# One loop over all eight head groups on TensorE, VectorE and ScalarE of a cached-attention decode kernel

## The chip, the cores and the metric

One core of a Trainium2 chip runs the kernel. The metric is the device time of one execution in microseconds, as the median of several runs. The engines are named TensorE (PE in the profile; PEld is its weight load), VectorE (DVE), ScalarE (ACT), GpSimd (POOL) and SyncE (SP, which here issues nearly all DMAs). A profile also has the granted TensorE clock.

## What is computed

One decode step of a transformer block for four batch rows with one token each: adaptive layer norm from a condition `c`, attention over a cache of 4096 keys and values for 32 heads, and a gated MLP. The bytes are in the two caches (134 MB each, bf16).

```python
mod = (_silu(c) @ w_mod).reshape(c.shape[0], 6, 1, -1)      # sa, ca, ga, sb, cb, gb
h = _layernorm(x) * (1 + ca) + sa
# _A_ref: B, Sq, D = 4, 1, 512; H, Sk, Dh = 32, 4096, 128
q = (h @ wq).reshape(B, Sq, H, Dh).transpose(0, 2, 1, 3)
scores = einsum('bhqd,bhkd->bhqk', q, k_cache) * Dh ** (-0.5)
o = einsum('bhqk,bhkd->bhqd', softmax(scores), v_cache)
x = x + ga * (o.transpose(0, 2, 1, 3).reshape(B, Sq, H * Dh) @ wo)
h = _layernorm(x) * (1 + cb) + sb
# _B_ref: z = gelu(h @ w_in); z1, z2 = halves, z2 layer-normed
# (z1 * (w_sp * z2 + b_sp)) @ w_out
x = x + gb * _B_ref(h, ...)
```

## The kernel before

The 32 heads are eight groups `g` of four heads. A *quad* `i = 4 g + b` is one group of one batch row: its keys fill one SBUF tile `kt[i % 2]` of 128 partitions by 16,384 bf16 (4 MiB: 32 partitions for each head, 128 keys on each), its values one tile `vt[i % 2]`. There are 32 quads, and two buffers for K and two for V.

The prologue loads `w_mod` and `wq` into the two V buffers, computes the modulation, the first layer norm, and `qbc`, the queries of all heads repeated over the partitions: eight products into PSUM, each cast by ScalarE. Then come the quads. In the step of quad `i`:

- SP issues the load of K of quad `i+1` and of V of quad `i`, and in the third quad of a group (`b == 2`) the group's slice of `wo` into `wo_g`.
- `diagonal(i-2)`: four small fp32 products pick each head's own block out of `osb`, the P.V result of quad `i-2`.
- `scores(i, half)`, twice: VectorE multiplies half of the K tile in place with the query (8192 elements a partition, 4.4 us), and TensorE adds the products up in groups with 16 products by the identity into a PSUM bank `s_ps[half]`.
- `project(i-2)`, between the halves: VectorE divides by the sum of exponentials `z`, into `oT`.
- `fold(i, half)`: VectorE's last reduction of the score sums into `S`.
- `softmax(i)`: maximum over each head (with two 32x32 transposes), Exp on ScalarE, and `P4`, the exponentials masked by head.
- `values(i-1)`: `z` by one fp32 product, then 32 products of P by V into `po_ps`; ScalarE copies that to `osb`.
- `apply(i-2)`, for the last quad of a group only: the product of the group's four `oT` with `wo_g`, added up in one PSUM bank `attn_ps`.

After the last quad `values_last` multiplies P and V in 128 small products, quad by quad of keys as the parts of the last V tile land, and goes to `attn_ps` with `wo_l`; then come the second layer norm, the MLP (weights `win`, `wout`) and the output.

Nothing is scheduled by a compiler. `Program` records each operation with the regions that it reads and writes, derives the waits (`depend`, `order`), and writes each engine's stream in recorded order (`run`). Each operation may raise one semaphore. Only TensorE has a loop: a pass is four quads, `passno = (i - 2) // B`, seven passes over quads 2 to 29; quads 0, 1, 30 and 31 are written out. TensorE inside its loop may wait only on semaphores whose names begin with `pe_`, since those counts repeat in every pass: at the end of a pass TensorE lowers each by what the pass added (five of them: `pe_act`, `pe_dve`, `pe_v0`, `pe_v1`, `pe_wo`). An operation whose exact predecessor raises no semaphore that it may read waits for a later one on the same engine that does (line 115). VectorE, ScalarE and SP are written out for all 32 quads.

The end has its own arrangements. For quad 31 the K tile is loaded in two halves with semaphores of their own (`load_k`, lines 400 to 405), so that the first half can be multiplied before the second lands; the V tile comes in five parts (`load_v`). `keep_busy(4)` puts four idle products ahead of the last scores (lines 645 to 646). `softmax(30)` is recorded after the products of quad 31 instead of in its own quad (lines 651 to 656). The six loads of late weights (`wo_l`, `win`, `wout`) are issued behind the V parts; `load_sp` lets loads whose names begin with `wo` or `wi` wait for the load eight places earlier in SP's stream.

Of the kernel before, what the change touches and what calls it, by code (L numbers as in the profile page):

```python
# [30 lines left out]
class Op:  # L31
    def __init__(self, eng, emit, reads, writes, sem, passno, done):
        self.eng, self.emit, self.reads, self.writes = eng, emit, reads, writes
        self.sem, self.passno, self.done = sem, passno, done
        self.pos = self.count = None
        self.clock, self.waits, self.dma = {}, [], False


class Program:
# [3 lines left out]
    def __init__(self, nc):  # L43
        self.nc = nc
        self.ops, self.by_eng = [], {}
        self.passno = None
        self.last_write, self.readers = {}, {}

    def add(self, eng, emit, reads, writes, sem=None, done=True, dma=False, after=()):
        reads, writes = list(reads), list(writes)  # L50
        for r in reads[:]:
            if r.space == bass.MemoryType.PSUM:
                reads.remove(r)
                writes.append(r)
        op = Op(eng, emit, [region(r) for r in reads], [region(w) for w in writes],
                sem or eng, self.passno, done)
# [9 lines left out]
    def depend(self, op):  # L66
# [7 lines left out]
        for r in op.reads:  # L74
            for w, reg in self.last_write.get(r[0], ()):
                if hit(r, reg):
                    deps.add((w, "raw"))
# [7 lines left out]
        for r in op.reads:  # L85
            self.readers.setdefault(r[0], []).append((op, r))
# [13 lines left out]
    def order(self):  # L100

        known = {}
        for op in self.ops:
# [6 lines left out]
            for key, d in sorted(need.items(), key=lambda kd: -kd[1].idx):  # L110
                if clock.get(key, -1) >= d.pos:
                    continue
                if not d.dma:
                    lst = self.by_eng[d.eng]
                    d = next(o for o in lst[d.pos:] if o.done and self.tells(o.sem, op))
                op.waits.append(d)
                for k, v in d.clock.items():
                    clock[k] = max(clock.get(k, -1), v)
            op.clock = dict(clock)
            op.clock[("dma", id(op)) if op.dma else op.eng] = op.pos  # L120
            if not op.dma:
                clock[(op.eng, "issued")] = op.pos

    def tells(self, sem, op):

        own = sem.startswith("pe_")
        return op.eng == "PE" and (own or op.passno is None) or op.eng != "PE" and not own

    def call(self, eng, name, *args, sem=None, done=True, after=(), **kw):
        outs = [kw[k] for k in OUTS if k in kw]  # L130
        ins = [v for k, v in kw.items() if k not in OUTS and isinstance(v, bass.AP)]
        if not outs:
            outs, args_in = [args[0]], args[1:]
            ins += [a for a in args_in if isinstance(a, bass.AP)]
        return self.add(
            eng, lambda e: getattr(e, name)(*args, **kw), ins, outs, sem=sem, done=done, after=after,  # L136
        )

    def load(self, eng, sem, out, in_, after=()):
        return self.add(  # L140
            eng, lambda e: e.dma_start(out=out, in_=in_), [], [out], sem=sem, dma=True, after=after,  # L141
        )

    def run(self, alloc, passes, engines):


        self.order()
        sems, total, count = {}, {}, {}
        for op in self.ops:
            if op.done:  # L150
                step = 16 if op.dma else 1
                total[op.sem] = total.get(op.sem, 0) + step
                op.count = total[op.sem]
                sems.setdefault(op.sem, None)
        for name in sems:
            sems[name] = alloc(name)
        loops = [[o for o in self.by_eng["PE"] if o.passno == p] for p in range(passes)]
        own = {s for s in sems if s.startswith("pe_")}
        step, wait = {}, []
        for pos in range(len(loops[0])):  # L160
            vals = [{d.sem: d.count for d in lp[pos].waits} for lp in loops]
            for v in vals:
                assert set(v) <= own, v
            wait.append(vals)
        for s in own:
            rows = [
                (p, pos, wait[pos][p][s]) for pos in range(len(wait)) for p in range(passes)
                if s in wait[pos][p]
            ]
            per = {}  # L170
            for p, pos, v in rows:
                per.setdefault(pos, {})[p] = v
            diffs = {
                (b - a) // 1 for d in per.values() for p in range(passes - 1)
                if p in d and p + 1 in d for a, b in ((d[p], d[p + 1]),)
            }
            assert len(diffs) <= 1, (s, diffs)
            step[s] = diffs.pop() if diffs else 0
        norm = []
        for pos, vals in enumerate(wait):  # L180
            best = {}
            for p, v in enumerate(vals):
                for s, x in v.items():
                    best[s] = max(best.get(s, 0), x - p * step[s])
            norm.append(best)

        def emit(op, eng, waits):
            waits = list(waits)
            for s, v in waits[1:]:
                eng.wait_ge(sems[s], v)  # L190
            inst = op.emit(eng)
# [4 lines left out]

        def plain(op):
            best = {}
            for d in op.waits:
                best[d.sem] = max(best.get(d.sem, 0), d.count)  # L200
            return best.items()

        for name, lst in self.by_eng.items():
            if name != "PE":
                for op in lst:
                    for d in op.waits:
                        assert d.sem not in own, (name, d.sem)
                    emit(op, engines[name], plain(op))
        pe = engines["PE"]
        seen = [o for o in self.by_eng["PE"] if o.passno is None]  # L210
        first = loops[0][0].pos
        for op in seen:
            if op.pos < first:
                emit(op, pe, plain(op))
        with pe.Fori(0, passes):
            for op, w in zip(loops[0], norm):
                emit(op, pe, w.items())
            for s in sorted(own):
                if step[s]:
                    pe.sem_inc(sems[s], -step[s])  # L220
        for op in seen:
            if op.pos > first:
                emit(op, pe, [(s, v - passes * step.get(s, 0)) for s, v in plain(op)])
# [3 lines left out]
def kernel(  # L227
# [111 lines left out]
    prog = Program(nc)  # L339
# [10 lines left out]
    def mm(out, lhsT, rhs, start, stop, done=False, **kw):  # L350
        prog.add(
            "PE", lambda e: e.matmul(out, lhsT=lhsT, rhs=rhs, start=start, stop=stop, **kw),  # L352
            [lhsT, rhs], [out], done=done,
        )

    def mm2(out, lhsT, rhs, start, stop, done=False):

        prog.add("PE", lambda e: e.ldweights(lhsT), [lhsT], [], done=False)  # L358
        moving(out, lhsT, rhs, start, stop, done)

    def moving(out, lhsT, rhs, start, stop, done=False):
        def emit(e):
# [7 lines left out]
        prog.add("PE", emit, [rhs], [out], done=done)  # L370
# [5 lines left out]
    prog.load("ACT", "rows_c", rows[0:B], c)  # L376
    prog.load("ACT", "rows_x", rows[B:2 * B], A_x.rearrange("b s d -> (b s) d"))
    prog.load("ACT", "wb_w", wb_t[:, 0:1], B_w_sp[0:1, 0:1])
    prog.load("ACT", "wb_b", wb_t[:, 1:2], B_b_sp.rearrange("(a b) -> a b", b=1))
    tables = "natural_log_exp_and_others"  # L380
    prog.add("ACT", lambda e: e.preload_act_table_set(tables), [], [], done=False)
# [3 lines left out]
    prog.load("SP", "wm", wm, w_mod.rearrange("(p j) n -> p (j n)", j=J))  # L385
    prog.load("SP", "wq", wq, A_wq.rearrange("(p j) n -> p (j n)", j=J))
# [7 lines left out]
    sp_dma = []  # L394

    def load_sp(sem, out, in_):
        near_end = sem[:2] in ("wo", "wi")
        sp_dma.append(prog.load("SP", sem, out, in_, after=sp_dma[-8:-7] if near_end else ()))

    def load_k(i):  # L400
        a = 0
        for n, part in enumerate((2, 2) if i == NQ - 1 else (1,)):
            b = a + NT * DH // part
            load_sp(f"k{i % 2}" if i < NQ - 1 else f"kl{n}", kt[i % 2][:, a:b], kv_view(A_k_cache, i)[:, a:b])
            a = b

    def load_v(i):
        a = 0
        for n, part in enumerate((2, 4, 8, 16, 16) if i == NQ - 1 else (1,)):
            b = a + NT * DH // part  # L410
            load_sp(
                f"pe_v{i % 2}" if 1 <= i <= 28 else f"v{i}_{n}",
                vt[i % 2][:, a:b], kv_view(A_v_cache, i)[:, a:b],
            )
            a = b

# [5 lines left out]
    for t in (wide, mask4, P4s[0], P4s[1], mxs[0], mxs[1]):  # L422
# [3 lines left out]
    dve("memset", ones_b, 1.0)  # L426
    dve("memset", ones_f, 1.0)
# [4 lines left out]

    def keep_busy(n):
        for _ in range(n):
            mm(big[1], ident, wide, True, True)
# [74 lines left out]
    mm(cut(attn_b, J * B), ident, wide[:, 0:J * B], True, True, skip_group_check=True)  # L510

# [3 lines left out]

    def scores(i, half):
        g, b = divmod(i, B)
        kh = view(kt[i % 2])[:, half * HT:(half + 1) * HT, :]
        dve(
            "tensor_tensor", out=kh, in0=kh,  # L520
            in1=qbc[:, b, g, :][:, None, :].to_broadcast([P, HT, DH]), op=MULT, sem="pe_dve",
        )
        n = DH // DC
        for cc in range(n):
            (mm2 if cc == 0 else moving)(
                s_ps[half], ident, kh[:, :, cc * DC:(cc + 1) * DC], cc == 0, cc == n - 1, cc == n - 1,
            )

    def fold(i, half):
        dve(  # L530
            "tensor_reduce", out=S_t[i % 2][:, half * HT:(half + 1) * HT], in_=s_ps[half],
            axis=AX.X, op=ADD,
        )

    def softmax(i):
# [3 lines left out]
        dve("tensor_reduce", out=mx[:, 0:1], in_=S, axis=AX.X, op=ALU.max)  # L539
# [237 lines left out]
```

## Time and profile before

| | |
|---|---|
| median of 3 runs | 667.03 us (666.99 to 667.08) |
| the profiled execution | 666.79 us, its span 665.0 us |
| busy: TensorE, VectorE, ScalarE | 417.8, 402.7, 41.2 us |
| mean granted TensorE clock | 0.77 |
| HBM read | 282.73 MB |
| K tile, from issue to landing (median) | 25.4 us |
| V tile, from issue to landing (median) | 33.1 us |

The span is what the profile covers; 1.8 us of the execution lie around it. In the timeline each line gives start, duration, engine, line and operation, the tiles written and read, how many, and in brackets the idle time of the engine before it and what ended that. All recorded operations other than matmuls carry the helper's line, so tiles tell them apart.

### The profile page before, as it was taken

What the parts mean: (1) busy time and instruction counts of PE and PEld (TensorE: products, weight loads), DVE (VectorE), ACT (ScalarE), POOL (GpSimd) and SP (SyncE); (2) the same over time, 40 slices, a digit from 0 to 9 for tenths busy, and PEclk for the clock granted to TensorE, in tenths of its full rate; (3) what the DMA queues carried; (4) which work ended last, traced back from release to release, by engine and by line L of the source; (5) the groups of instructions that cost most, each with busy time, mean ns of one, the idle gap of its engine ahead of it and who ended that gap; (6) DMA issues with size and microseconds to landing.
All of it is one profiled execution on the core that took longest, in us unless ns stands there. A gap on an engine that the chain in (4) does not pass through costs nothing.

```text
span 665.0 us, 5909 instructions
## 1 busy us (share of the span) xinstructions
PE 417.8 (63%) x3024; PEld 93.0 (14%) x2065; DVE 402.7 (61%) x475; ACT 41.2 (6%) x115; POOL 3.2 (0%) x17
## 2 busy tenths in 40 slices
PE   2657777565577754576655667656547675567774
PEld 2201111011110101111001111101111110112124
DVE  2166777676556666555766655757655666655662
ACT  1200000000000000000000000000000000000002
POOL 1000000000000000000000000000000000000000
PEclk9977777677887767888766788766778766788895
DMA  9999999999999999999999999999999999999995
GB/s 379 428 424 440 437 422 434 439 434 428 434 436 430 434 434 436 424 436 433 439 428 434 440 426 434 436 434 430 430 440 436 426 434 438 434 430 432 431 416 218
DMA packets 12673, 282.90 MB, mean 425 GB/s; under 512 B 1388, under 2 KB 1908, under 8 KB 3956
## 3 DMA queue, kind: packets, MB, share of 16 engines
q1 hardware_dynamic: 12640, 282.73, 98.8%
q8 instruction: 7, 0.11, 0.1%
q14 instruction: 6, 0.05, 0.0%
q10 hardware_dynamic: 20, 0.01, 0.0%
HBM read 282.73 MB, written 0.00 MB: 425 GB/s over the span
## 4 chain that ended last, share of the span: by engine, by line
DMA 62%; PE 24%; DVE 12%; issue 0%; SPq 0%; ACT 0%; DVEq 0%
DMA kt<-in_A_k_cache_dram 58%; PE bank L363 24%; DVE kt L136 11%; DMA vt<-in_A_v_cache_dram 3%; DMA wout<-in_B_w_out_dram 1%; PE bank L352 0%; SPq L141 0%; DVE S L136 0%; DVE P L136 0%; ACT E L136 0%; DVE mx L136 0%; DVE nm L136 0%; DVE mT L136 0%; DVE hm L136 0%; DVE hb L136 0%
## 5 line engine op out<-in xcount | busy, mean ns | idle before, releaser
L363 PE MATMUL bank<-kt,ident 128*128 128x512 bf16 x1024 | 293.0, 457 | 179.7 <-DVE kt L136 179.7
L136 DVE TENSOR_TENSOR kt<-kt,qbc 128x8192 bf16<-128x8192 bf16 x64 | 282.7, 4419 | 84.7 <-DMA kt<-in_A_k_cache_dram 84.6
L136 DVE TENSOR_REDUCE S<-bank 128x64 f32<-128x512 f32 x64 | 44.2, 691 | 123.9 <-PE bank L363 123.9
L352 PE MATMUL bank<-vt,P 128*32 128x512 bf16 x992 | 59.2, 380 | 1.5 <-DMA vt<-in_A_v_cache_dram 1.5
L358 PEld LDWEIGHTS <-ident 128*128 128x128 bf16 x64 | 9.1, 142 | 356.2 <-issue 356.1
L352 PE MATMUL bank<-sel,osb 128*128 128x4 f32 x248 | 34.2, 261 | 29.4 <-ACT osb L136 24.9
L136 ACT ACTIVATE E<-S,nm 128x128 f32<-128x128 f32 x32 | 12.8, 401 | 561.9 <-DVE nm L136 561.9
L352 PEld LDWEIGHTS bank<-sel,osb 128*128 128x128 f32 x248 | 31.5, 199 | 41.9 <-ACT osb L136 36.8
L136 DVE TENSOR_TENSOR P<-E,mask 128x512 bf16<-128x512 f32 x32 | 22.1, 692 | 17.9 <-ACT E L136 17.9
L352 PEld LDWEIGHTS bank<-vt,P 128*32 128x32 bf16 x992 | 23.6, 96 | 22.3 <-DMA vt<-in_A_v_cache_dram 1.6
L352 PEld LDWEIGHTS bank<-rs,ones_f 128*128 128x128 f32 x64 | 12.1, 190 | 104.8 <-issue 100.7
L136 ACT COPY osb<-bank 128x512 f32<-128x512 f32 x31 | 17.5, 565 | 20.0 <-PE bank L352 20.0
L352 PE MATMUL bank<-vt,hbc 128*32 128x512 bf16 x128 | 9.9, 485 | 4.7 <-DMA vt<-in_A_wq_dram 4.7
L136 DVE RECIPROCAL rz<-bank 128x4 f32<-128x4 f32 x32 | 5.6, 175 | 8.1 <-PE bank L352 8.1
L352 PE MATMUL bank<-oP,wo_g 128*128 128x4 bf16 x112 | 3.9, 165 | 10.2 <-DVE oP L136 10.2
L136 DVE TENSOR_REDUCE mx<-S 128x1 f32<-128x128 f32 x32 | 9.1, 286 | 1.1
L352 PE MATMUL bank<-rs,ones_f 128*128 128x4 f32 x64 | 9.1, 212 | 0.0
L136 DVE STREAM_TRANSPOSE nm<-hb 128x32 f32<-128x32 f32 x32 | 6.8, 212 | 1.1
L136 DVE STREAM_TRANSPOSE mT<-mx 128x32 f32<-128x32 f32 x32 | 6.8, 212 | 1.1
L136 DVE TENSOR_SCALAR rs<-mask,rs 128x4 f32<-128x4 f32 x32 | 7.1, 223 | 0.0
L136 DVE TENSOR_REDUCE hm<-mT 128x1 f32<-128x32 f32 x32 | 5.9, 186 | 1.1
L136 DVE TENSOR_SCALAR hb<-hm 128x32 f32<-128x32 f32 x32 | 5.8, 181 | 1.1
(91 smaller groups left out, 75.6 us busy)
## 6 DMA issues: line engine op xcount, KB each, us to landing
kt<-in_A_k_cache_dram SPq DMA_DIRECT2D x31, 4096.0 KB, 25.4
vt<-in_A_v_cache_dram SPq DMA_DIRECT2D x31, 4096.0 KB, 33.1
vt<-in_A_wq_dram SPq DMA_DIRECT2D x1, 4096.0 KB, 20.2
kt<-in_A_k_cache_dram SPq DMA_DIRECT2D x2, 2048.0 KB, 25.7
wo_g<-in_A_wo_dram SPq DMA_DIRECT2D x7, 512.0 KB, 21.9
vt<-in_w_mod_dram SPq DMA_DIRECT2D x1, 3072.0 KB, 9.9
vt<-in_A_v_cache_dram SPq DMA_DIRECT2D x1, 2048.0 KB, 19.0
win<-in_B_w_in_dram SPq DMA_DIRECT2D x1, 1344.0 KB, 14.5
```

The lines of the kernel that those rows point to most:

```text
L136: eng, lambda e: getattr(e, name)(*args, **kw), ins, outs, sem=sem, done=done, after=after,
L352: "PE", lambda e: e.matmul(out, lhsT=lhsT, rhs=rhs, start=start, stop=stop, **kw),
L358: prog.add("PE", lambda e: e.ldweights(lhsT), [lhsT], [], done=False)
L363: return e.add_instruction(mybir.InstMatmult(name=nc.get_next_instruction_name(), engine=mybir.EngineType.PE, ins=[e.lower_ap(rhs), e.lowe ...
```

## The change

TensorE, VectorE and ScalarE each run one loop of eight passes, one for each head group, over four quads. The recording is now regular: every pass has the same operations, with `passno = g`.

*Zero quads.* Quad -2 and quad -1 are thereby part of the first pass: `diagonal(-2)`, `project(-2)`, `values(-1)`, `diagonal(-1)`, `project(-1)` and `apply(-1)` run on zeros. GpSimd sets `oT`, `wo_g` and `osb_t[0]` to zero, VectorE sets `rs4_t[1]` to one, and one more small product fills the bank of `z` of quad -2. `values(-1)` reads P4 (zeros) and `vt[1]`, which then holds `wq`, so that V of quad 1 is loaded after it.

*Semaphores.* Each is named for who may wait on it and who raises it: `pe_dve`, `dve_pe`, `act_dve`, `sp_pe` and so on, or `any_...` outside the loops. Each operation in the loops names its one reader with `sem=`: the last `scores` product VectorE, the `z` product and the first product of `diagonal` SP, the last of `values` ScalarE, the last of `diagonal` VectorE. SP, which isn't looped, thus waits for the `z` product where it waited for the last `scores` product, and for `diagonal`'s first product (or the last of `apply`) where it waited for the last of `values`; `load_v(i)` is recorded after `diagonal(i-2)`.

*Gate.* What operations in the loop need from ahead of it is waited for once, before the loop: on VectorE and TensorE all of GpSimd's setup and all eight casts of `qbc`.

*Addresses.* VectorE's product reads `qbc[:, b, g, :]` with `g` from the loop's register; one register instruction per quad computes the address.

*The end.* After the loops stand `diagonal(30)`, `project(30)`, the last P.V (written out in place) and what follows. K of quad 31 is one load. `keep_busy` is gone. `softmax(30)` stands in its own quad. The late weights are recorded after the loops; the first three wait for the first part of the last V tile, the others for the second, third and fourth.

```diff
-        for name, lst in self.by_eng.items():
-            if name != "PE":
...
-        with pe.Fori(0, passes):
-            for op, w in zip(loops[0], norm):
-                emit(op, pe, w.items())
-            for s in sorted(own):
-                if step[s]:
-                    pe.sem_inc(sems[s], -step[s])
+        for name, lst in self.by_eng.items():
+            eng = engines[name]
+            if name not in self.looped:
...
+            for s, v in newest(self.gate.get(name, ())).items():
+                eng.wait_ge(sems[s], v)
+            for s in own:
+                if bias[s]:
+                    eng.sem_inc(sems[s], bias[s])
+            with eng.Fori(0, passes) as it:
+                for op, w in zip(loops[0], norm):
+                    emit(op, eng, [(s, v + bias[s]) for s, v in w.items()], it)
+                for s in own:
+                    eng.sem_inc(sems[s], -step[s])
...
-    prog = Program(nc)
+    prog = Program(nc, ("PE", "DVE", "ACT"))
...
     def load_k(i):
-        a = 0
-        for n, part in enumerate((2, 2) if i == NQ - 1 else (1,)):
-            b = a + NT * DH // part
-            load_sp(f"k{i % 2}" if i < NQ - 1 else f"kl{n}", kt[i % 2][:, a:b], kv_view(A_k_cache, i)[:, a:b])
-            a = b
+        prog.load("SP", f"dve_k{i % 2}", kt[i % 2], kv_view(A_k_cache, i))
...
-    for t in (wide, mask4, P4s[0], P4s[1], mxs[0], mxs[1]):
+    for t in (wide, mask4, P4s[0], P4s[1], mxs[0], mxs[1], oT, wo_g, osb_t[0]):
         pool("memset", t, 0.0)
...
         dve(
-            "tensor_tensor", out=kh, in0=kh,
-            in1=qbc[:, b, g, :][:, None, :].to_broadcast([P, HT, DH]), op=MULT, sem="pe_dve",
+            "tensor_tensor", out=kh, in0=kh, op=MULT, sem="pe",
+            dyn=lambda g: {"in1": qbc[:, b, g, :][:, None, :].to_broadcast([P, HT, DH])},
         )
...
     for i in range(NQ):
-        prog.passno = (i - 2) // B if 2 <= i < 2 + B * PASSES else None
         g, b = divmod(i, B)
+        prog.passno = g
...
-        if i > 1:
-            diagonal(i - 2)
-        if i == NQ - 1:
-            keep_busy(4)
+        diagonal(i - 2, "dve")
+        v_done = load_v(i)
         scores(i, 0)
-        if i > 1:
-            project(i - 2)
+        project(i - 2, "dve")
         scores(i, 1)
-        if i == NQ - 1:
-            softmax(i - 1)
         fold(i, 0)
         fold(i, 1)
-        if i != NQ - 2:
-            softmax(i)
-        if i > 0:
-            values(i - 1)
-        if i > 1:
+        softmax(i)
+        values(i - 1)
+        if b == 1:
             apply(i - 2)
     prog.passno = None
-    diagonal(NQ - 2)
-    project(NQ - 2)
-    values_last(NQ - 1)
-    project(NQ - 1)
+    late = [(wo_l[a], wo_v[G - 1, :, a * NH // 2:(a + 1) * NH // 2]) for a in range(2)]
+    late += [(win[a], win_v[:, j0:j1, :]) for a, (j0, j1) in enumerate(WJS)]
+    late += [(wout[a], wout_v[a]) for a in range(2)]
+    for n, (t, src) in enumerate(late):
+        prog.load("SP", f"any_late{n}", t, src, after=[v_done[max(n - 2, 0)]])
...
```

## The prediction

> **What bounds the kernel now.** I read the page first, then the answers of the timeline for the start, a middle quad and the end, then the windows, then the records of landing DMAs. (A quad is one step `i`: four heads of one batch row, one 4 MiB K tile and one 4 MiB V tile.) The page:
>
> ```profile
> span 665.0 us, 5909 instructions
> ...
> GB/s 379 428 424 440 437 422 434 439 434 428 434 436 430 434 434 436 424 436 433 439 428 434 440 426 434 436 434 430 430 440 436 426 434 438 434 430 432 431 416 218
> ...
> q1 hardware_dynamic: 12640, 282.73, 98.8%
> q8 instruction: 7, 0.11, 0.1%
> q14 instruction: 6, 0.05, 0.0%
> ...
> L136 DVE TENSOR_TENSOR kt<-kt,qbc 128x8192 bf16<-128x8192 bf16 x64 | 282.7, 4419 | 84.7 <-DMA kt<-in_A_k_cache_dram 84.6
> ```
>
> The loads run at one rate from the second slice to the last but one; 8.39 MB a quad at 433 GB/s is 19.4 us, and 32 quads are 620 us of 665. VectorE stands idle 84.6 us for K tiles; without the first wait (13.7 us) that is 71 us over 28 quads, 2.5 us a quad. So the compute chain of a quad takes some 17 us of 19.4, and this 2.5 us is what a new cost in the middle must exceed. A middle quad and its K issue:
>
> ```profile
> 587.85 0.33 SPq L141 DMA_DIRECT2D kt<-in_A_k_cache_dram  x1
> ...
> 592.78 4.43 DVE L136 TENSOR_TENSOR kt<-kt,qbc 128x8192 bf16<-128x8192 bf16 x1 [1.59 <-DMA kt<-in_A_k_cache_dram]
> ...
> 606.09 0.69 DVE L136 TENSOR_REDUCE S<-bank 128x64 f32<-128x512 f32 x1 [2.76 <-PE bank L363]
> ...
> 608.46 0.56 ACT L136 COPY osb<-bank 128x512 f32<-128x512 f32 x1
> ```
>
> The K tile issued at 587.85 lands at 612.1, 24.3 us later, though 4 MiB last 9.7 us: about 14 us of older loads stand ahead of it. An issue that comes a few us late therefore costs nothing here. The end:
>
> ```profile
> 632.46 4.42 DVE L136 TENSOR_TENSOR kt<-kt,qbc 128x8192 bf16<-128x8192 bf16 x1
> ...
> 647.00 1.77 PE L352 MATMUL bank<-P,vt 128*128 128x4 bf16 x64 [0.97 <-DMA vt<-in_A_v_cache_dram]
> ...
> 652.63 0.17 DVE L136 TENSOR_TENSOR oT<-bank,rz 128x4 bf16<-128x4 f32 x1
> ...
> 653.72 0.17 DVE L136 TENSOR_TENSOR x1b<-bank,modT 128x16 f32<-128x16 f32 x1 [0.92 <-PE bank L363]
> ...
> 660.00 0.49 PE L363 MATMUL bank<-u,wout 128*128 128x12 bf16 x12 [0.16 <-DMA wout<-in_B_w_out_dram]
> ```
>
> All of this waits for DMA: the last P.V chunks for V31, `x1b` for `wo_l`, the last product for `wout`; but the MLP chain follows within 0.2 us. Whatever delays the last attention step by more than that shows in full.
>
> **The change, part by part.**
>
> *Middle.* New per pass of four quads: on VectorE five semaphore decrements, a register add, a branch, and four register instructions for the address of `qbc`. TensorE closes such a loop in the kernel before, also with five decrements; from the end of `apply` (137.74+0.55) to `diagonal` (138.95) are 0.66 us. I take 0.66 us plus four times at most 0.1 (no row shows the register instruction; the smallest VectorE row, 0.06 us, and 0.2 us for any small tensor operation bound it): about 1 us per pass, hidden by 4 × 2.5 = 10 us of waiting for K; without this cover 8 × 1 = 8 us. ScalarE's loop end (two decrements) hides in its waits of 16 us a quad; TensorE's now follows `values` and hides in the wait of `diagonal` for `osb` (1.07 us in row 590.85), where before it stood bare. SP: a K issue now waits for the `z` product behind `scores` (+0.3 us), a V issue for `diagonal`'s first product, which waits for ScalarE's copy behind Exp: 590.8 instead of 589.8, and up to 2.6 us where `apply` stands between. SP is in order, so the next K is behind it, but that comes 16 us later. The 14 us cover these. Cost 0; both ends 0 and +0.5.
>
> *Start.* VectorE passes a gate that waits for all eight casts of `qbc`: the last ends at 31.60+0.58 = 32.18, the first product now starts at 31.29 with K0's landing. +0.9, and 0.05 to 0.66 us for entering the loop (the loop end above as upper bound). Then +0.3 for the `z` product: K2 is issued 1.3 to 1.9 us after 45.43. Issued by then were 19.9 MB (3 MiB `w_mod`, four tiles of 4 MiB); the windows add up to 18.6 MB moved, 1.3 MB or 3.1 us left, with K2's bytes following about 1.2 us after issue (first issue 0.97, the windows show bytes from 2.0). So the margin is 1.9 us for the average DMA engine, more for the late ones: cost 0, upper bound 0.5. The zero quads add TensorE work (`values(-1)` 1.9 us, two `diagonal` of 1.05, an `apply` of 0.8) where TensorE idled (7.75 us before row 53.15), and V1 is issued 5 us later, behind a K2 that lasts 9.7. GpSimd's three more memsets (2.1 us for `wo_g` by the 0.53 of `wide`) end near 8 us, long before 32. Cost 0.
>
> *End.* The last K tile is no longer split, TensorE isn't warmed by `keep_busy`, and `softmax(30)` goes back to its own quad (into idle time). So both products start at the landing of the whole tile, L = 632.46 in this trace, where one is now done by then. From product to second fold took 13.3 (592.78 to 606.09), 13.9 and 14.4 us in the quads before; over 17 quads of the chain of waits TensorE's part is 9.2 us mean, 8.4 to 10.0. I take 13.7: second fold F = 646.2. From F: `osb(30)` copied at F+2.93 (608.46+0.56−606.09), `diagonal` +0.05+1.05, `z` +0.35, the last P.V 128 × 27.7 ns (1.77/64) = 3.54 with all of V there, `oT` +0.22: F+8.1 = 654.3 against 652.8, +1.5. The 0.19 us that waited for `wo_l` and 0.2 for `wout` fall away: **+1.1 us**, from +0.3 (8.4) to +1.9 (10.0). The six late loads are issued up to 16 us later, each behind a landed part of V31, but always with at least 2 MB (5 us) queued: 0.
>
> *Instructions.* VectorE's stream falls from 474 listed instructions to 118, ScalarE's by more than half. In the landing records the last of 16 DMA engines ends 1.4 us behind the last but one at L (632.44, 631.01). Its lag grew by 0.7 us just after an instruction packet at 433.0 and by 1.0 us around one at 616.6. That of 433.0 is VectorE's: packets at 52, 236, 433 and 632 come each about 130 of its instructions after the last. A looped stream doesn't fetch it. So L comes 0 to 1.4 us earlier; I take **−0.7**.
>
> [...] The row first: TensorE branched back seven times over more than 500 instructions with a gap of 0.66 us and no instruction packet between 118 and 624 us on its queue. [...]
>
> Sum: 0 + 0 + 1.1 − 0.7 = +0.4. The profiled execution took 666.79 us (span 665.0 and 1.8 around it), 0.24 below the median of 667.03; on the median, **667.4 us**.
>
> **Rivals.**
> 1. *The unsplit last tile decides (slower).* L stays (the lag at 616.6 is the larger part and SP's or ScalarE's packet may remain), TensorE is slow (10.0: +1.9), one loop exit on the path (+0.5): +2.4, **669.4**. It decides from +1.3, that is when less than half of the lag goes. For: the tail's slack of 0.2 us. Against: the lag visibly tied to VectorE's fetch.
> 2. *Faster.* L 1.4 us earlier and warm TensorE (+0.3): −1.1; with `z` and `oT` overlapping better −1.5: **665.5**. Against: both ends at once.
> 3. *The branches fetch (slower).* Seven loop ends with one packet each, 0.7 us of lag as at 433: 7 × 0.7 = 4.9 on one engine, plus the tail's 1.1: **673**. For: VectorE's stream is fetched piecewise already. Against: TensorE's row.
>
> **How the numbers follow.** A median differs from no change if it is off by over 0.2%, 1.3 us. Forecast 0.55 (666.0 to 668.4), first rival 0.24, second 0.11, third 0.10. Range 665.8 to 670.3: it leaves out the third rival and half of the second. Faster 0.11; same 0.54; slower 0.35, the first and third with a little.
>
> **What would show it.** Right: K waits of VectorE still over 50 us in sum, GB/s at 430 in slices 3 to 38, the first VectorE product at 32.3 to 33, the last unsplit product 13 to 14.5 us before its second fold, `x1b` near 654 to 655, few q14 packets, 1.8 us outside the span. Wrong: VectorE never waiting for K, q14 with 10 packets or more, a dip of GB/s at 48 us or in the middle, or a gap of over 1.5 us at VectorE's loop ends with the K queue run dry.

## The result, and the profile after

| | before | after |
|---|---|---|
| median of 22 runs each | 666.96 us (666.77 to 667.21) | 665.87 us (665.41 to 666.78) |
| ratio | 1 | 0.9984, 95% interval 0.9978 to 0.9991 |
| the profiled execution, its span | 666.79, 665.0 us | 665.95, 664.2 us |
| first VectorE product that needs all of the last K tile, `L` | 632.46 us | 630.66 us |
| from `L` to the issue of the output | 29.67 us | 30.61 us |

The kernel became faster by 1.09 us. That is 0.16%, inside the 0.2% that the prediction called no measurable change; with 22 runs on each side the interval still excludes equality. The forecast was 667.4, a little slower; the measured median lies 0.07 us above the lower end of the range that was given, on the other side of no change.

The page after (span, bandwidth by slice, the three queues, VectorE's costliest group):

```profile
span 664.2 us, 6210 instructions
...
GB/s 379 418 432 440 434 423 436 442 420 432 442 432 426 436 442 420 432 442 428 431 436 442 422 430 442 432 426 436 442 420 432 442 434 424 436 442 420 432 422 230
...
q1 hardware_dynamic: 12496, 282.73, 98.9%
q8 instruction: 6, 0.10, 0.1%
...
q14 instruction: 2, 0.02, 0.0%
...
L159 DVE TENSOR_TENSOR kt<-kt,qbc 128x8192 bf16<-128x8192 bf16 x64 | 282.8, 4419 | 81.6 <-DMA kt<-in_A_k_cache_dram 81.6
```

The bandwidth in the middle is what it was (422 to 440 GB/s in slices 3 to 38 before, 420 to 442 after). VectorE still waits for K (81.6 us, 84.6 before), so the loop's overhead stays hidden. What is new is the line of q14, a queue that carries packets of instructions: two packets, where there were six. (The experiments show that VectorE's and ScalarE's come on q14 and TensorE's on q8: on their pages q14 has six packets with VectorE written out and seven with ScalarE written out and 32 more instructions a quad, and q8 has 20 with TensorE written out, for the two and six of this page.) The end, in the timeline:

```profile
630.66 4.42 DVE L159 TENSOR_TENSOR kt<-kt,qbc 128x8192 bf16<-128x8192 bf16 x1 [2.68 <-DMA kt<-in_A_k_cache_dram]
...
635.14 9.39 PE L386 MATMUL bank<-kt,ident 128*128 128x512 bf16 x32 [6.44 <-DVE kt L159]
...
644.58 0.69 DVE L159 TENSOR_REDUCE S<-bank 128x64 f32<-128x512 f32 x1 [2.76 <-PE bank L386]
...
652.29 0.17 DVE L159 TENSOR_TENSOR oT<-bank,rz 128x4 bf16<-128x4 f32 x1 [3.16 <-PE bank L376]
...
653.11 0.17 DVE L159 TENSOR_TENSOR x1b<-bank,modT 128x16 f32<-128x16 f32 x1 [0.66 <-PE bank L386]
...
661.27 0.36 SPq L731 DMA_DIRECT2D out_dram<-ot  x1
```

The last line of the kernel before, to compare:

```profile
662.13 0.36 SPq L732 DMA_DIRECT2D out_dram<-ot  x1
```

The last K tile lands 1.80 us earlier. The end behind it is 0.94 us longer, because both halves of the tile now start at its landing. -1.80 + 0.94 = -0.86; the profiled executions differ by -0.84.

Why does the tile land earlier? A 4 MiB tile has 16 landing records in the trace, read here as the end of each of the core's 16 DMA engines. This table, worked out from them for K of quad 31, is the key to the whole case ("lag" is the last engine's end behind the first's; the packets are those of instructions on q14 from 60 to 625 us):

```
                       q14 packets, us             first    last     lag
before                 218, 236, 433, 617          628.92   632.44   3.52
after                  none                        628.92   630.64   1.72
```

The first engine ends at the same time. Only the late engines differ. In the kernel before, the lag grew in steps: from 2.00 to 2.72 us in the tile that was moving at 433, and from 2.58 to 3.56 in that of 617. Between the two it stayed within 0.15 us for 180 us. The reading to be tested: an engine that carries a packet of instructions falls behind and has no idle time in which to catch up (q1's packets took 98.8% of the 16 engines' span before and 98.9% after); all of K 31 is awaited, so the latest engine sets `L`.

### The profile page after: what moved, and what is told of

It reads as the page before. It is cut to its first block, busy times and chain, and to the rows that moved or that the text cites. A ratio compares the mean times of both kernels' runs of the same rounds, so it can differ in the third digit from the quotient of the medians.

```text
span 664.2 us, 6210 instructions
## 1 busy us (share of the span) xinstructions
PE 421.6 (63%) x3104; PEld 93.8 (14%) x2144; DVE 403.3 (61%) x481; ACT 41.5 (6%) x116; POOL 5.7 (1%) x20
## 3 DMA queue, kind: packets, MB, share of 16 engines
q1 hardware_dynamic: 12496, 282.73, 98.9%
## 4 chain that ended last, share of the span: by engine, by line
DMA 58%; PE 26%; DVE 14%; issue 1%; ACT 1%; SPq 0%; ACTq 0%; DVEq 0%
DMA kt<-in_A_k_cache_dram 58%; PE bank L386 25%; DVE kt L159 12%; PE bank L376 1%; DVE S L159 0%; ACT E L159 0%; ACT L703 0%; DVE mx L159 0%; ACT rstd_ln L159 0%; DVE nm L159 0%; DVE mT L159 0%; SPq L165 0%; DVE hm L159 0%; DVE hb L159 0%; DVE rs L159 0%
## 5 line engine op out<-in xcount | busy, mean ns | idle before, releaser
L386 PE MATMUL bank<-kt,ident 128*128 128x512 bf16 x1024 | 297.4, 462 | 180.0 <-DVE kt L159 180.0
L159 DVE TENSOR_TENSOR kt<-kt,qbc 128x8192 bf16<-128x8192 bf16 x64 | 282.8, 4419 | 81.6 <-DMA kt<-in_A_k_cache_dram 81.6
L376 PE MATMUL bank<-vt,P 128*32 128x512 bf16 x1024 | 61.1, 380 | 0.0
L159 DVE TENSOR_TENSOR oT<-bank,rz 128x4 bf16<-128x4 f32 x34 | 5.7, 169 | 4.3 <-PE bank L376 3.2
```

The lines of the kernel that those rows point to most:

```text
L159: return getattr(e, name)(*args, **kw, **(dyn(it) if dyn else {}))
L376: "PE", lambda e, it: e.matmul(out, lhsT=lhsT, rhs=rhs, start=start, stop=stop, **kw),
L386: return e.add_instruction(mybir.InstMatmult(name=nc.get_next_instruction_name(), engine=mybir.EngineType.PE, ins=[e.lower_ap(rhs), e.lowe ...
```

## The experiments

Theory: written-out streams fetch packets of instructions, each packet puts one DMA engine behind, and the latest engine sets the time. The trace doesn't say which of the 16 engines carried a packet; what ties them is that a lag grows in the tile that moves at the packet's time. Rivals: the loops gain by the engines' own work; the early landing comes from the new order of SP's issues; the plain end costs something else than predicted. The experiments ran on several chips; the kernel before took 667.05 to 667.13 us beside them and 666.96 beside the change, so times of different groups compare to some 0.2 us, and each ratio is to the kernel before on its own chip.

**One part of the change undone.** Only the list of looped engines changes; with VectorE written out, the pass is that of the recording.

```diff
-    prog = Program(nc, ("PE", "DVE", "ACT"))
+    prog = Program(nc, ("PE", "ACT"))
```

> The changed kernel with VectorE written out again (TensorE and ScalarE looped, all else the same). Theory (each fetched block of an instruction stream holds up one of the 16 DMA engines by 0.5 to 1 us for good, and the last tile lands when the last engine is done): q14 has 4 to 5 packets where the changed kernel has 2, the lag of the last engine at the last K tile is between 1.7 and 3.5 us, and the median is 0 to 1.5 us above the changed kernel's 665.9, most likely 666.4. Rival (the gain comes from the rearranged end, the streams don't matter): 665.9, within 0.2. Rival (VectorE's loop costs something that is hidden by the gain): below 665.6.

Measured: 668.24 us (667.64 to 668.66), ratio to before 1.0015 (1.0006 to 1.0024), higher than expected. The q14 packets came back at 232.6, 420.0 and 613.3 us, and the lag stepped from 1.94 to 2.91 us at the second and from 2.74 to 3.73 at the third. (Of the six packets on the page's q14 line one, at 0.1 us, has only 104 bytes.) Page, then timeline:

```profile
q8 instruction: 6, 0.10, 0.1%
...
q14 instruction: 6, 0.04, 0.0%
```

```profile
632.76 4.42 DVE L161 TENSOR_TENSOR kt<-kt,qbc 128x8192 bf16<-128x8192 bf16 x1 [3.88 <-DMA kt<-in_A_k_cache_dram]
...
658.10 2.05 PE L388 MATMUL bank<-h,win 128*128 128x4 bf16 x56 [2.29 <-DMA win<-in_B_w_in_dram]
...
661.43 0.48 PE L388 MATMUL bank<-u,wout 128*128 128x12 bf16 x12 [0.18 <-DMA wout<-in_B_w_out_dram]
```

`L` is 2.10 us later than after, the last product was 0.71 us shorter, and the MLP's products wait for `win` and `wout`, which they didn't after (0.90 us). The wait for the weights doesn't follow from the lag alone: the next run has a longer one, and there these products wait for `h`. VectorE's loop alone is worth more than the whole change brought (0.31% of the time by the two ratios, 2.1 us), and both late packets are VectorE's. SP's new order of issues is still in this kernel, so it isn't what made the tile land early.

**VectorE and ScalarE written out.** `Program(nc, ("PE",))`.

> The changed kernel with VectorE and ScalarE both written out, TensorE alone looped. Theory (instruction blocks on DMA engines): packets on q14 as before the change (5 to 6), lag of the last engine at the last K tile 2 to 3.5 us, median 666.3 to 667.7. Rival (rearranged end): 665.9, within 0.2.

Measured: 668.07 us (667.44 to 669.37), 1.0015 (1.0006 to 1.0024), 0.4 us above the expected range. One packet more, at 218.6 us, so that one is ScalarE's; `L` 632.78, as with VectorE alone. Looping ScalarE is worth nothing that these runs can tell.

**The kernel before with the plain end.**

```diff
-        for n, part in enumerate((2, 2) if i == NQ - 1 else (1,)):
+        for n, part in enumerate((1,)):
...
-        if i == NQ - 1:
-            keep_busy(4)
...
-        if i == NQ - 1:
-            softmax(i - 1)
...
-        if i != NQ - 2:
-            softmax(i)
+        softmax(i)
```

> The kernel before with the changed kernel's end alone: the last K tile in one load, no idle products, softmax of quad 30 in its own quad. Theory (the end costs, the streams gain): 0.7 to 1.9 us slower than before, 668.0, with the last K tile landing near 632.4 and its second fold 13 to 14.5 us later. Rival (the rearranged end is the gain): 0.5 to 1.1 us faster than before, 665.9 to 666.5.

Measured: 667.99 us (667.68 to 668.73), 1.0016 (1.0007 to 1.0025): +0.9 us, as expected in sum, though not by the end alone. Timeline:

```profile
632.85 4.43 DVE L136 TENSOR_TENSOR kt<-kt,qbc 128x8192 bf16<-128x8192 bf16 x1 [3.53 <-DMA kt<-in_A_k_cache_dram]
637.33 9.02 PE L363 MATMUL bank<-kt,ident 128*128 128x512 bf16 x32 [7.29 <-DVE kt L136]
...
655.09 0.17 DVE L136 TENSOR_TENSOR x1b<-bank,modT 128x16 f32<-128x16 f32 x1 [0.66 <-PE bank L363]
...
663.22 0.36 SPq L727 DMA_DIRECT2D out_dram<-ot  x1
```

From `L` to `x1b` are 22.24 us, 0.98 more than the 21.26 before, and from `L` to the output's issue 30.37, 0.70 more than the 29.67. The other 0.39 us of this execution are a later landing: the lag is 3.92 us for 3.52, with the same number of q14 packets. The run with VectorE and ScalarE written out is the same in time: zero quads, new semaphores, gate and TensorE's longer loop cost nothing that these runs can tell.

**The changed kernel with odd K tiles in halves,** to have the earlier start of the last tile back inside a regular loop.

```diff
-        prog.load("SP", f"dve_k{i % 2}", kt[i % 2], kv_view(A_k_cache, i))
+        if i % 2 == 0:
+            prog.load("SP", "dve_k0", kt[0], kv_view(A_k_cache, i))
+            return
+        for n in range(2):
+            cols = slice(n * HT * DH, (n + 1) * HT * DH)
+            prog.load("SP", f"dve_k1{n}", kt[1][:, cols], kv_view(A_k_cache, i)[:, cols])
```

> The changed kernel with every odd K tile loaded in two halves, each with a semaphore of its own, so that the first half of the last tile can be multiplied before the second lands. Theory (what is left of the end is the chain behind the last K tile, which was late by the landing of a whole tile): the last P.V then waits for the last part of V instead, x1b 0.3 to 0.6 us earlier, median 665.2 to 665.6 and a smaller spread of the runs, since the TensorE clock of the last scores no longer shows. Rival (the last tile's split costs nothing or gains nothing): 665.9, within 0.2.

Measured: 666.14 us (665.99 to 666.49), 0.9986 (0.9977 to 0.9995): a miss, no gain over the changed kernel. Only the smaller spread came, 0.5 us for 1.4. Timeline:

```profile
651.94 0.17 DVE L159 TENSOR_TENSOR oT<-bank,rz 128x4 bf16<-128x4 f32 x1 [3.42 <-PE bank L376]
...
652.81 0.37 PE L386 MATMUL bank<-oT,wo_l 128*128 128x4 bf16 x8 [0.30 <-DMA wo_l<-in_A_wo_dram]
653.22 0.17 DVE L159 TENSOR_TENSOR x1b<-bank,modT 128x16 f32<-128x16 f32 x1 [1.12 <-PE bank L386]
```

`oT` is 0.35 us earlier than after, but the product with `wo_l` now waits for its DMA. This run's lag was 2.18 us too.

**More packets without more work.** ScalarE written out, with 12 or 32 extra instructions a quad on it: waits on a count that was reached long ago. As a control, the 32 inside ScalarE's loop: executed as often, hardly fetched (one q14 packet from 60 to 625 us, for five written out). And TensorE written out, the other two looped. The line added in the control; the written-out ones also have `("PE", "DVE")` as the looped engines, and one of them 12 for 32:

```diff
         act("copy", out=osb_t[i % 2], in_=po, sem="pe")
+        prog.add("ACT", lambda e, it: [e.wait_ge(sems["any_rows_c"], 16) for _ in range(32)], [], [], done=False)
```

> The changed kernel with ScalarE written out and 12 extra instructions a quad on it (waits that are long satisfied): some 384 more listed instructions, which at 128 to an 8 KB packet are three more packets on q14, and one for the written-out stream itself. Theory (each packet of instructions puts one of the 16 DMA engines behind for good, by 0.5 to 1.1 us, and the last engine sets the landing of the last K tile): 5 to 7 q14 packets instead of 2, the last engine 2.3 to 3.7 us behind the first at the end instead of 1.7, K31 at 631.3 to 632.7, time 666.6 to 668.2. Rival (VectorE's loop gains by VectorE's own work, not by packets): the packets come, the time stays at 665.4 to 666.4.

> The same with 32 extra instructions a quad, some 1024 more in the stream: eight or nine more packets on q14. Theory: 9 to 12 q14 packets, lag of the last engine 3 to 5 us, K31 at 632 to 634, time 667.3 to 669.5, above the run with 12. Rival: 665.4 to 666.4 whatever the number of packets. If the packets hit 16 engines in turn, the time grows with the number of packets less than in proportion.

> Control: the same 32 extra instructions a quad are executed, but inside ScalarE's loop, so that the stream holds only about 128 more (one packet of 8 KB). Theory: 2 to 4 q14 packets, lag 1.7 to 2.5 us, time 665.5 to 666.7, as the changed kernel. Rival (executing the extra instructions costs, not fetching them): as high as the run with 32 written out.

> The changed kernel with TensorE written out and the other two looped: about 542 instructions a pass, 8 passes, at 256 to a 16 KB packet some 17 packets on q8 instead of 6, each lasting 0.95 us instead of 0.31. Theory: the last engine 3.5 to 5.5 us behind the first at the last K tile, K31 at 632.5 to 634.5, time 667.7 to 670, though no engine has more to do. Rival (only VectorE's fetches cost, since VectorE then stands still): 665.2 to 666.4, TensorE having slack in the middle.

Measured, beside the others with both halves starting at `L`. `d` is TensorE's part of the last product in the timeline; `T` is the profiled execution:

```
                          packets 60-625 us              L       d     T       T-L-d   median (range)
                          q14  q8   first   last    lag
after                      0   2   628.92  630.64  1.72  630.66  9.39  665.95  25.90   665.87 (665.41-666.78)
12 more, written out       2   2   629.01  630.99  1.99  631.02  9.24  666.15  25.89   665.98 (665.64-666.87)
32 more, in the loop       1   2   629.00  631.20  2.20  631.22  9.07  666.19  25.90   666.19 (665.62-666.93)
32 more, written out       5   2   629.09  632.43  3.34  632.46  8.49  667.28  26.33   667.28 (666.74-667.95)
VectorE written out        3   2   629.00  632.73  3.73  632.76  8.68  668.24  26.80   668.24 (667.64-668.66)
VectorE, ScalarE w. out    4   2   628.85  632.76  3.91  632.78  8.95  667.76  26.03   668.07 (667.44-669.37)
before, plain end          4   2   628.91  632.83  3.92  632.85  9.02  667.89  26.02   667.99 (667.68-668.73)
TensorE written out        0  16   628.96  633.95  4.99  633.98  9.60  670.73  27.15   670.61 (670.05-670.73)
```

The first engine ends within 0.25 us in all eight; the lag orders the times, but for three kernels within 0.25 us of each other. The 32 extra instructions cost 1.4 us over the changed kernel where they are written out and 0.3 (inside the spread) where they are looped: 1.1 us between two kernels that execute the same instructions, for 1.14 us of lag. So fetching them costs, and executing them doesn't, as far as these runs can tell. The timeline of the last K product, first of the written-out kernel, then of the control:

```profile
632.46 4.42 DVE L161 TENSOR_TENSOR kt<-kt,qbc 128x8192 bf16<-128x8192 bf16 x1 [2.21 <-DMA kt<-in_A_k_cache_dram]
```

```profile
631.22 4.42 DVE L159 TENSOR_TENSOR kt<-kt,qbc 128x8192 bf16<-128x8192 bf16 x1 [3.01 <-DMA kt<-in_A_k_cache_dram]
```

Two expectations missed in a way that teaches. With 12 more, the packets at 121.9 and 394.9 us came and the time stayed, which is what the rival said of that run: in the sorted list of 16 lags one value moved from 0.49 to 1.14 us at the first, while the last stayed at 1.99. In these runs a packet cost time where it left its engine later than all others, and none that can be told where it didn't. (With 32 more, three packets moved the last engine by 0.15 us together; those at 473.7 and 613.3 raised it from 2.15 to 2.81 and from 2.71 to 3.37.) The number of packets alone, which both expectations on written-out waits started from, was also too high: five between 60 and 625 us, not eight or nine. (Their 128 instructions to a packet of 8 KB, and the 256 to one of 16 KB for TensorE, are the author's estimates. In the trace of the kernel before, 132 and 122 of VectorE's listed instructions lie between its packets of 8 KB at 236, 433 and 617 us, and 253 to 259 of TensorE's between its first four of 16 KB; for the waits added here the estimate did not hold.)

With TensorE written out the lag was as expected, the time 0.6 us above. Page and timeline:

```profile
q8 instruction: 20, 0.33, 0.2%
q14 instruction: 2, 0.02, 0.0%
```

```profile
633.98 4.43 DVE L161 TENSOR_TENSOR kt<-kt,qbc 128x8192 bf16<-128x8192 bf16 x1 [2.45 <-DMA kt<-in_A_k_cache_dram]
...
656.01 0.13 PEld L383 LDWEIGHTS <-wo_l 128*128 128x128 bf16 x2 [0.40 <-issue]
657.35 0.42 PEld L383 LDWEIGHTS <-wo_l 128*128 128x128 bf16 x13 [1.21 <-issue]
```

`T-L-d` is 1.25 us longer than after. That is the gap of 1.21 us in the middle of the products with `wo_l`, where TensorE waits for nothing that the profile shows, with a packet of its instructions at 654.9 that is over before the gap begins. Whether it waited for instructions there stays open; no run tested it.

**A version that takes both.** Seven passes looped, the last head group written out on the three engines, once with the old end of the kernel before (K of quad 31 in halves, the four idle products, the softmax of quad 30 behind them) and once with the plain one; and the changed kernel again on the same chip.

```diff
-        prog.passno = g
+        prog.passno = g if g < G - 1 else None
...
-        prog.run(alloc, G, {
+        prog.run(alloc, G - 1, {
```

> The changed kernel with seven passes instead of eight on the three engines; the last head group is written out and has the end of the kernel before again: K of quad 31 in two halves, four idle products ahead of its scores, the softmax of quad 30 behind its products. Theory (time is the lag of the last DMA engine plus the end): the end gives back 0.9 us; against it stand two or three 16 KB packets of TensorE's and perhaps one 8 KB packet of VectorE's between 550 and 632 us, free if they hit early engines (lag 1.7 to 2.2: 665.0 to 665.5), 1 us dearer if one hits the last engine (lag 2.7 to 3.2: 666.0 to 666.5). Rival (as with the odd K tiles in halves, the last weights then arrive last and hold the end): no gain over the changed kernel even at a lag of 2, 665.8 to 666.5.

> Seven passes and the last group written out, but with the plain end of the changed kernel. Theory: only the late packets are new: 665.9 if none of them hits the last engine, up to 667.2 if one does; 0.9 above the run with the old end at the same lag. Rival: equal to the run with the old end.

> The changed kernel as it is, on the same chip as the two others: 665.5 to 666.3, two q14 packets, the last engine again 1.7 to 2.2 us behind the first at the last K tile. If the lag is a matter of where packets happen to fall, it differs from the first profile and the time with it, 1 us for 1 us.

Measured: with the old end 665.64 us (665.49 to 665.78), ratio 0.9978 (0.9969 to 0.9987); with the plain end 666.25 (665.46 to 667.04), 0.9987 (0.9978 to 0.9996); the changed kernel 666.12 (665.58 to 667.01), 0.9989 (0.9980 to 0.9998). The first is the best kernel of the study by its median, 0.5 us below the changed kernel on the same chip, although the two intervals overlap. The plain end is 0.6 us above the old one, where 0.9 was expected. The timeline with the old end:

```profile
626.46 4.43 DVE L164 TENSOR_TENSOR kt<-kt,qbc 128x8192 bf16<-128x8192 bf16 x1 [0.38 <-DMA kt<-in_A_k_cache_dram]
...
631.30 4.42 DVE L164 TENSOR_TENSOR kt<-kt,qbc 128x8192 bf16<-128x8192 bf16 x1
...
645.82 1.76 PE L381 MATMUL bank<-P,vt 128*128 128x4 bf16 x64 [0.97 <-DMA vt<-in_A_v_cache_dram]
...
652.16 0.38 PE L391 MATMUL bank<-oT,wo_l 128*128 128x4 bf16 x8 [0.32 <-DMA wo_l<-in_A_wo_dram]
...
660.99 0.36 SPq L747 DMA_DIRECT2D out_dram<-ot  x1
```

`L` is 1.16 us earlier than before, and from `L` to the output's issue are 29.69 us against 29.67: the kernel before, with its lag of 3.52 us down to 2.30. A packet of TensorE's at 606.4 raised the last engine from about 2.0 to 2.33. The plain end beside it has `L` 630.99, lag 2.10, `d` 9.44, `T` 666.38, so `T-L-d` is again 25.95.

The second profile of the changed kernel, in its timeline:

```profile
631.06 4.42 DVE L159 TENSOR_TENSOR kt<-kt,qbc 128x8192 bf16<-128x8192 bf16 x1 [1.81 <-DMA kt<-in_A_k_cache_dram]
635.54 8.57 PE L386 MATMUL bank<-kt,ident 128*128 128x512 bf16 x32 [5.58 <-DVE kt L159]
...
660.89 0.36 SPq L731 DMA_DIRECT2D out_dram<-ot  x1
```

The lag is 2.01 us, 0.3 more than in the first, `d` 8.57 and `T` 665.58: `T-L-d` is 25.95 again. With its lag this execution was expected to be later, 1 us for 1 us, and was earlier: `d` was 0.82 us shorter. (The median of the 11 runs is 0.25 us above that of the 22.) The windows show what differed (after first, then the second profile; the columns are stretch, length, busy time of PE, PEld, DVE, ACT and POOL, granted clock, DMA share, GB/s):

```profile
635.00:640.00 5.00, 4.86 (x12) 0.00 (x0) 4.68 (x4) 0.00 (x0) 0.00 (x0) 0.51 0.94 403
640.00:645.00 5.00, 5.00 (x31) 0.71 (x15) 1.11 (x2) 0.00 (x0) 0.00 (x0) 1.00 0.96 411
```

```profile
635.00:640.00 5.00, 4.46 (x14) 0.00 (x0) 4.97 (x4) 0.00 (x0) 0.00 (x0) 0.64 0.98 419
640.00:645.00 5.00, 5.00 (x38) 0.92 (x23) 1.62 (x4) 0.00 (x0) 0.00 (x0) 1.00 0.96 410
```

TensorE had stood idle for 6.44 and 5.58 us. In the 5 us in which the last product starts, the granted clock is 0.51 in one profile and 0.64 in the other; in the next 5 us it is 1.00 in both. (In the kernel before, with `keep_busy` and the first half's products ahead, it is 0.66 from 630 to 635 us and 1.00 from 635 to 640; no run took the idle products away alone.) How much of the product falls into the slow part is the likely source, which no run tested by itself, of the spread of this kernel: its runs lie within 1.4 us of each other, those of the plain end beside it within 1.6. With the old end they lie within 0.3. There half of the tile is multiplied ahead, and the P.V products wait for parts of V (0.97 us in the row at 645.82), so up to that much of a slower product is covered by the landing of V.

## Why the prediction was wrong, by its own steps

- *Middle, 0:* right. At the loop end behind quad 7 VectorE's last operation of the pass, `rs`, ends at 176.29, and the next product starts with the landing of K, 2.78 us later; at all seven loop ends the wait for K is 1.95 to 3.26 us, and the overhead is inside it. VectorE written out brought packets and no gain.

```profile
176.07 0.22 DVE L159 TENSOR_SCALAR rs<-mask,rs 128x4 f32<-128x4 f32 x1
179.08 4.42 DVE L159 TENSOR_TENSOR kt<-kt,qbc 128x8192 bf16<-128x8192 bf16 x1 [2.78 <-DMA kt<-in_A_k_cache_dram]
```

- *Start, 0:* right, by other numbers. The casts of `qbc` ended earlier, the last at 31.37 (32.18 before), so the first product starts with K0's landing at 31.34 (31.29 before) and not 0.9 later, and K2 was issued at 44.66, ahead of the 45.43 before and not 1.3 to 1.9 us behind it:

```profile
30.79 0.58 ACT L159 CAST qbc<-bank 128x512 bf16<-128x512 f32 x1 [0.28 <-PE bank L376]
31.34 4.42 DVE L159 TENSOR_TENSOR kt<-kt,qbc 128x8192 bf16<-128x8192 bf16 x1 [13.94 <-DMA kt<-in_A_k_cache_dram]
...
44.66 0.33 SPq L165 DMA_DIRECT2D kt<-in_A_k_cache_dram  x1
```

- *End, +1.1:* right in kind, and inside its bounds but once. Measured 0.94 in the change itself and 0.70 in the kernel before with the plain end, but 0.16 in the second profile of the changed kernel (29.83 us from `L` to the output's issue): it isn't one price, it goes with `d`. `d` was 9.39, 9.02 and 8.57 us. With the 9.2 that was taken, the 25.9 us of `T-L-d` give +0.8. After the change, from `L` to the second fold were 13.92 us where 13.7 were taken, and the end of `oT` came 7.88 us behind the fold for the 8.1 predicted.
- *Instructions, -0.7, bound 0 to -1.4:* **this is the step that failed.** The mechanism was right, the size wrong: -1.80 in the profiled execution, -1.40 in the second profile of the same kernel, whose lag was 0.3 us longer; either is at least twice the term. Two things made it small. The prediction gave the packet at 433 to VectorE and left the larger step, at 617, open to SP or ScalarE; so it took half. With VectorE alone written out both steps come back (420.0 and 613.3), and ScalarE's own packet is that of 218. VectorE's fetches were those at 236, 433 and 617; the packets at 52 and 632, which the prediction counted with them in place of 617, are still there with VectorE looped (51.5 and 633.6). And the bound was the distance to the last but one engine, which was itself late by 0.4 us more before (2.09 behind the first) than after (1.69). How much of that comes from the streams and how much from one execution to the next stays open: in the second profile the last but one was 1.81 behind, and the last 2.01.
- *TensorE's row, and VectorE's branches:* as TensorE's branches back had brought no packet on q8 between 118 and 624 us before, the seven of VectorE brought none on q14 between 60 and 625 us, and it was the straight-line stream that cost 2.1 us (VectorE written out, by the two ratios). The waits of VectorE that the trace of the kernel before lists are for K (84.6 us) or for another engine, none for instructions; what came late were the DMA engines (a lag of 3.52 us), and this kernel is bound by them (98.8% of their span, by q1's line). (TensorE's row in the prediction stands for six branches back, not seven, since seven passes branch back six times.)
- *The sum:* 0 + 0 + 0.94 - 1.80 = -0.86 in the profiles, for +0.4. The profiled executions moved by 0.84; that of before lay 0.17 us below its median and that of after 0.08 above, so the medians moved by 1.09. With the end as predicted and the landing 1.4 to 1.8 us earlier the sum would have been faster, not slower.
- *The rivals:* "the unsplit last tile decides" fell: its condition was that less than half of the lag goes. "Faster" came true at 665.87 for its 665.5, by the early landing, though with a slower last product than it asked for (9.39 us, not 8.4). That its number is so near is luck: the landing was 0.4 us better than its end and the end 0.6 worse. "The branches fetch" fell: fewer packets, not more. Its one packet at each of seven loop ends was an assumption of the author's that no run shows; with VectorE looped q14 had none there.

## What to carry to other kernels

Where the DMA engines are as busy as here (98.9% of their span after), look at the spread of the 16 engines' landings, not only at the mean bandwidth: most of the difference between these kernels was in the latest engine (a lag of 1.72 us after, 3.73 with VectorE written out, 4.99 with TensorE), and a step in its lag at the time of an instruction packet (0.66 to 0.99 us for VectorE's and ScalarE's) was the price of a written-out stream. When a trace shows several such steps, settle which engine's stream each packet belongs to (by instruction counts, or by looping one engine at a time) before taking a part of them. And keep a special end outside the loop if it shortens the path behind the last load: seven looped passes and a written-out last group kept the early landing and the old end, 0.5 us below the changed kernel by the medians on one chip.

## What the runs showed that was not expected

- One packet of 8 KB, which takes 0.31 us by itself, put an engine 0.65 to 1.0 us behind where the step could be followed; one of 16 KB (0.88 us) up to 1.5 (3.57 to 5.07 us of lag at 587 us, TensorE written out). The engine then stayed behind: 2.72 us after the packet at 433 us, 2.58 at 612.
- `T-L-d` was 25.89 to 26.03 us for the five kernels of the table whose end waited for nothing else, and 25.95 in both later profiles of the plain end. The exceptions are waits for late weights (0.4 and 0.9 us more, but none in two other kernels with a lag of 3.9 us) and the gap with TensorE written out.
- A lag of 1.8 to 2.2 us was there by 100 us in every kernel; no run here removed it, and where it comes from stays open.
